# Turning all dS units by DMA and giving one dS product in sixteen to GpSimd

## The chip, the cores and the metric

The kernel runs on one core of a Trainium2 chip. A core has a matrix engine (TensorE, "PE"), three engines for elementwise work (VectorE "DVE", ScalarE "ACT", GpSimd "POOL"), a queue engine that here only issues transfers (SyncE, "SP"), and 16 DMA engines that carry out the transfers of all queues. The metric is the device time of one execution in microseconds; a time stands for the median of several runs. A profiled execution adds a record of every instruction and of every DMA packet.

## The reference

The program computes one transformer block and all its gradients. Sequence length 2048, width 512, 32 heads of 16 columns, an MLP of width 1792 with squared ReLU, and six modulation vectors from a condition vector. Cut to what matters here:

```python
def attention(x, wqkv, wo):                    # B=1, S=2048, H=32, Dh=16
    q, k, v = split_heads(x @ wqkv)
    scores = einsum('bhqd,bhkd->bhqk', q, k) * Dh ** -0.5
    p = softmax(scores)
    o = einsum('bhqk,bhkd->bhqd', p, v)
    return merge_heads(o) @ wo

out, vjp = jax.vjp(block, x, wqkv, wo, w1, b1, w2, b2, c, w_mod)
grads = vjp(grad_out)                          # nine gradients
```

The backward pass of attention makes, for each head, the probabilities E again, the product dP = dO V^T, the gradient dS = E * dP (the row terms of the softmax ride along in padded rows of the operands), and from these dV = E^T dO, dK = dS^T Q and dQ = dS K.

## The kernel before

The forward pass and the MLP fill the first 1120 us or so. The change lies in what follows, the backward loop of attention (lines 1554 to 1763).

**Units.** The 32 heads are taken four at a time (8 head groups). A unit is one head group, one chunk of 512 keys (`kc`), one chunk of 512 queries (`qc`), and one tile of 128 of these queries (`qi`); there are 512 units, and four consecutive ones (the four `qi`) are a block, 128 blocks in all. Queries lie on the partitions, keys along the free dimension.

**Steps of a unit.** `score` (line 1588): for each of the four heads, PE multiplies q by k into one PSUM bank of 128x512; three banks, called A, B and C, take turns. `expo` (1598): ACT takes the exponential of that bank into a quarter of `E_u` (bf16, 128x2048; four such buffers). `dp_pair` (1603): for two heads at a time, PE makes dP in the two-bank PSUM tile `psD_u` (two buffers), and DVE multiplies it by E into half of `dS_u` (bf16, 128x2048, six buffers); two such products of 128x1024 make a unit's dS. `k_quad` and `v_quad` (1644, 1653): PE adds dS^T q and E^T dO into the bank `accVK`. `transpose_unit` (1622): SP issues a DMA transpose of the whole `dS_u`, 512 KB, into a quarter of `dsT`, a tile per block (three buffers). `dq_quad` (1669): two blocks later PE multiplies the turned dS by K into `dqacc`, which shares bank C, and `dq_out` (1680) lets ACT copy it and POOL add it to the dQ of the head group.

**The fourth unit of every second block.** For blocks with odd number (`on_pe`), the unit with `qi == 3` is not turned by DMA. Instead `pe_turn` (1636) has PE turn it by 16 matmuls of 128x128 with the identity, eight at a time into `ptT` in bank C, and ACT copies each eight into `dsT` (line 1756, 128x1024). So 448 units are turned by DMA and 64 by PE.

**Order.** The loop is scheduled by hand on all five engines: a string of tokens for each block gives the order in which instructions are issued, and each engine works through its own in that order. `s` is a score, `e` an exp, `D` a `dp_pair`, `q` a `k_quad` or `v_quad` in turn, `d` two `dq_quad`s of the block two back, `Q` its `dq_out`; `t` and `T` are the PE turn and its copy, `f` a dummy matmul on PE (`keep_warm`, 1632). There are two strings: `order_t` in the blocks that follow an odd one, with `t`, `T` and four `f`, and `order_n` in the others. A unit's transpose is issued with its second `D`. `at` hangs the loads of the next head group on ACT's queue, one at every fourth `D`, and, at the end of the loop, five loads on SP's queue.

Of the kernel before, what the change touches and what calls it, by code (L numbers as in the profile page):

```python
# [14 lines left out]
AF = mybir.ActivationFunctionType  # L15
ALU = mybir.AluOpType
AX = mybir.AxisListType
BF = dt.bfloat16
F32 = dt.float32

P = 128
D = 512
# [12 lines left out]
def kernel(  # L35
# [17 lines left out]
    PE = nc.tensor  # L53
    DVE = nc.vector
    ACT = nc.scalar
    POOL = nc.gpsimd
# [5 lines left out]
    identb = persist.tile([P, P], BF, name="identb")  # L62
# [84 lines left out]
    with ExitStack() as ph:  # L147
# [4 lines left out]
        ework = att.enter_context(tc.tile_pool(name="phCe", bufs=4))  # L152
# [1048 lines left out]
        def head_fill(i):  # L1201
            for key in ("k", "v", "q", "do"):
                POOL.memset(hsets[i][key][:], 1.0 if key in ("k", "v") else 0.0)
# [345 lines left out]
    with ExitStack() as ph:  # L1549
        tpool = ph.enter_context(tc.tile_pool(name="phIt", bufs=3))  # L1550
        ework = ph.enter_context(tc.tile_pool(name="phIe", bufs=4))
        wk = ph.enter_context(tc.tile_pool(name="phIw", bufs=2))
        psd = ph.enter_context(tc.tile_pool(name="psId", bufs=2, space=bass.MemoryType.PSUM))
        psx = ph.enter_context(tc.tile_pool(name="psIx", bufs=1, space=bass.MemoryType.PSUM))
        units = [(hg, kc, qc, qi) for hg in range(HG) for kc in range(QC) for qc in range(QC) for qi in range(4)]
        NU = len(units)
        hst, bst, sst, dqt, cur = {}, {}, {}, {}, {}

        def load_head(hg):
            st = dict(hsets[hg % 2])  # L1560
            st["qz"] = qz[hg % 2]
            st["acc"] = stg.tile([P, n], F32, name="dQacc", tag="dQacc", bufs=1)
            st["dq"] = stg.tile([P, n], BF, name="dQst", tag="dQst", bufs=1)
            st["vk"] = stg.tile([P, n], BF, name="vkb", tag="vkb")
            hst[hg] = st
# [22 lines left out]
        def score(u, hq, bank):  # L1588
            hg, kc, qc, qi = units[u]
            st = hst[hg]  # L1590
            qt = qc * 4 + qi
            r = 32 * hq
            psS = psx.tile([P, 512], F32, name=f"psS_{bank}", tag=banks[bank])
            sst[u, hq] = psS
            PE.matmul(psS[:], st["q"][r:r + 32, qt * P:(qt + 1) * P], st["k"][r:r + 32, kc * 512:kc * 512 + 512],  # L1595
                      start=True, stop=True, tile_position=(r, 0))

        def expo(u, hq):
            if hq == 0:
                bst[u] = [ework.tile([P, 4, 512], BF, name="E_u", tag="E_u"), None]  # L1600
            ACT.activation(bst[u][0][:, hq, :], sst.pop((u, hq))[:], AF.Exp, scale=SCALE)  # L1601

        def dp_pair(u, pair):
            hg, kc, qc, qi = units[u]
            st = hst[hg]
            qt = qc * 4 + qi
            if pair == 0:
                bst[u][1] = ework.tile([P, 4, 512], BF, name="dS_u", tag="dS_u", bufs=6)
            E_u, dS_u = bst[u]
            psD = psd.tile([P, 2, 512], F32, name="psD_u", tag="pd")  # L1610
            for hi in range(2):
                r = 32 * (2 * pair + hi)
                PE.matmul(psD[:, hi, :], st["do"][r:r + 32, qt * P:(qt + 1) * P], st["v"][r:r + 32, kc * 512:kc * 512 + 512],  # L1613
                          start=True, stop=True, tile_position=(r, 0))
            DVE.tensor_tensor(dS_u[:, 2 * pair:2 * pair + 2, :], psD[:], E_u[:, 2 * pair:2 * pair + 2, :], ALU.mult)  # L1615
            if qi == 3 and on_pe(u // 4):
                held["dS"] = dS_u

        def on_pe(b):
            return b % 2 == 1  # L1620

        def transpose_unit(u):
            hg, kc, qc, qi = units[u]
            if qi == 0:
                dqt[u // 4] = tpool.tile([P, 4, 16, P], BF, name="dsT", tag="dsT")
            if qi == 3 and on_pe(u // 4):
                return
            SP.dma_start(out=dqt[u // 4][:, qi], in_=bst[u][1].rearrange("p h k -> p (h k)"), transpose=True)

        held = {}  # L1630

        def keep_warm():
            PE.matmul(cur["vk"][0:DH, :], KS_tok[:, 0, D:QPAD], dOs_tok[:, 0, :], start=False, stop=False,
                      tile_position=(0, 0), skip_group_check=True)

        def pe_turn(b, half):
            pt = psx.tile([P, 8, P], BF, name="ptT", tag="px")
            for i in range(8):
                kt = i % 4
                PE.transpose(pt[:, i, :], held["dS"][:, 2 * half + i // 4, kt * P:(kt + 1) * P], identb[:])  # L1640
            dst = dqt[b][:, 3, 8 * half:8 * half + 8, :]
            held[half] = (dst, pt)

        def k_quad(u):
            hg, kc, qc, qi = units[u]
# [34 lines left out]
        def dq_out(b):  # L1680
# [17 lines left out]
                    r = hg % 2 * 64 + hq * DH  # L1698
                    at(cur["j"] + 6 + hq, load, dQc[hg // 2, r:r + DH, :], st["dq"][32 * hq:32 * hq + DH, :])

        order_t = (
# [3 lines left out]
            "s15 q q e15 ").split(), "ABCABBABACABABCA"  # L1705
        order_n = (
            "s0 D s1 q e0 q s2 e1 e2 D s3 s4 q s5 e3 D e4 "
            "e5 s6 q s7 D s8 e6 e7 d1 e8 s9 D d2 e9 q Q s10 "
            "s11 e10 D q s12 e11 e12 s13 e13 D q s14 s15 e14 e15 D q ").split(), "CBACBACBABABCABC"
# [6 lines left out]
        with tc.manual_schedule(engines={PE.engine, ACT.engine, DVE.engine, SP.engine, POOL.engine}):  # L1716
            head_fill(1)
            POOL.memset(qz[1][:], 0.0)
            nD, nq = -1, -4
            idle = psx.tile([P, 512], F32, name="idle", tag="accVK")  # L1720
            for b in range(NU // 4 + 3):
                toks, bank = order_t if on_pe(b - 1) else order_n
                for tok in toks:
                    c, i = tok[0], int(tok[1:] or 0)
                    if c == "s" and b < NU // 4:
                        if i == 0 and units[4 * b][1:] == (0, 2, 0) and units[4 * b][0] + 1 < HG:
                            load_head(units[4 * b][0] + 1)
                        score(4 * b + i // 4, i % 4, bank[i])
                    elif c == "e" and b < NU // 4:
                        expo(4 * b + i // 4, i % 4)  # L1730
                        if b < 2 and i % 2 == 1:
                            if nq > 0:
                                keep_warm()
                            elif nq < 0:
                                PE.matmul(idle[:], ones_bf[:], identb.unsqueeze(1).to_broadcast([P, 4, P]), start=True, stop=True)
                    elif c == "D":
                        if 0 <= nD < 2 * NU:
                            dp_pair(nD // 2, nD % 2)
                            if nD % 2 == 1:
                                transpose_unit(nD // 2)  # L1740
                        nD += 1
                        cur["j"] = nD
                        for j in sorted(j for j in todo if j <= nD):
                            for f, args in todo.pop(j):
                                f(*args)
                    elif c == "q":
                        if 0 <= nq < 2 * NU:
                            (v_quad if nq % 2 else k_quad)(nq // 2)
                        nq += 1
                    elif c == "f" and 0 < nq < 2 * NU:  # L1750
                        keep_warm()
                    elif c == "t" and 0 <= b - 1 < NU // 4:
                        pe_turn(b - 1, i - 1)
                    elif c == "T" and 0 <= b - 1 < NU // 4:
                        dst, pt = held.pop(i - 1)
                        ACT.activation(dst, pt[:], AF.Identity)  # L1756
                    elif c == "d" and 0 <= b - 2 < NU // 4:
                        for kt in (2 * i - 2, 2 * i - 1):
                            dq_quad(b - 2, kt)
                    elif c == "Q" and 0 <= b - 2 < NU // 4:  # L1760
                        dq_out(b - 2)
            assert not todo
        dq_last = hst[HG - 1]["dq"]

    with ExitStack() as ph:
# [15 lines left out]
        order = (("vk", 6), ("vk", 0), ("vk", 1), ("vk", 2), ("vk", 3), ("dq", 0), ("vk", 7), ("dq", 1), ("vk", 4), ("dq", 2), ("vk", 5), ("dq", 3))  # L1781
# [140 lines left out]
        with tc.manual_schedule(engines={PE.engine, ACT.engine, DVE.engine}):  # L1922
            for k, (key, i) in enumerate(order):
                for g in range(2):
                    if (2 * k + g) % 2 == 0:
                        pt = pst.tile([P, 8, P], BF, name="ptq", tag="ptq")
                    else:
                        pt = psd.tile([P, 8, P], BF, name="ptd", tag="pdh1")
                    for ti in range(8):
                        t = 8 * g + ti  # L1930
                        PE.transpose(pt[:, ti, :], xs[key, i][:, t * P:(t + 1) * P], identb[:])
                    if key == "dq":
                        dst = dq_tok[:, 8 * g:8 * g + 8, i * P:(i + 1) * P]
                    else:
                        dst = dvk_tok[:, 8 * g:8 * g + 8, i, :]
# [32 lines left out]
            for b in range(3):  # L1968
                for ic in range(DC):
                    dwqkv(b, ic)  # L1970
                    i = b * DC + ic
# [75 lines left out]
```

## Time and profile before

| What | Value |
|---|---|
| Median of three runs | 2543.87 us (2539.78 to 2545.97) |
| Span of the profiled execution, first to last instruction | 2533.7 us |
| The profiled execution's own time | not listed apart from its span |
| Backward loop, first to last transpose issued | 1126.1 to 2401.7 us |
| PE busy | 2353.2 us, 93% |
| ACT busy | 2305.1 us, 91% |
| DVE busy | 1808.8 us, 71% |
| POOL busy | 348.5 us, 14% |
| Packets of SP's DMA queue (q1) | 81.9% of the 16 engines' span |

The page has the busy share of each engine over the whole span, rows of 40 slices of equal length (63.3 us each) with a digit for the tenths that an engine was busy, the granted clock of PE and the busy share of the DMA engines in the same slices, the DMA queues with their packets, the chain of work that ended last, and the costliest groups of instructions. "SPq" is SP's queue of DMA issues. On DVE and ACT an instruction's listed time begins while the one before it is still draining, so the time an instruction takes from its engine is read from start to start. Further answers of the trace give a line's or a tile's instructions with their shortest, middle and longest time, a timeline of an engine in which like instructions without idle time between them are merged into one piece, the busy times in a stretch, and who waited for whom.

### The profile page before, as it was taken

The page shows a single profiled execution, that of the slowest core. Times are in us where ns is not written, and L with a number is a line of the kernel's source. Part 1 is how long each engine was busy: PE and PEld are TensorE (multiplying, and loading weights), DVE is VectorE, ACT ScalarE, POOL GpSimd, SP SyncE. Part 2 cuts the span into 40 slices and gives each one's busy share as a digit, 9 for nine tenths or more (in the row PEclk, how much of TensorE's full clock was granted, in tenths as well). Part 3 has the DMA queues.
Part 4 walks back from the last instruction along what each step waited for, and adds up shares of the span by engine and source line. Part 5 has one row for each costly group of instructions (what it writes and reads, how often), then busy time and mean ns, then how long its engine had stood idle before and what let it go on. Part 6 is the DMA issues. An engine that isn't in the chain of part 4 may idle for free.

```text
span 2533.7 us, 50560 instructions
## 1 busy us (share of the span) xinstructions
PE 2353.2 (93%) x19005; PEld 777.5 (31%) x19005; DVE 1808.8 (71%) x2317; ACT 2305.1 (91%) x3577; POOL 348.5 (14%) x370
## 2 busy tenths in 40 slices
PE   7898889989988998999999999999999999999999
PEld 3232223223322323533232223232232322332343
DVE  5555153454444455579899999899998998998872
ACT  7999999999999999549999999999999998998952
POOL 2000001211323141110101101011010110100100
PEclk9999999999999999999899999999999999999999
DMA  6477454366649765979999999999999999999972
GB/s 204 126 191 190 140 130 128 90 164 144 94 101 193 129 144 119 276 199 194 189 201 199 198 197 203 197 195 201 206 202 195 202 195 199 202 203 207 200 241 73
DMA packets 1227131, 447.21 MB, mean 177 GB/s; under 512 B 1103096, under 2 KB 1197752, under 8 KB 1226631
## 3 DMA queue, kind: packets, MB, share of 16 engines
q1 hardware_dynamic: 1198966, 409.14, 81.9%
q0 software_dynamic: 10944, 16.78, 4.6%
q10 hardware_dynamic: 16976, 18.07, 2.6%
q8 instruction: 149, 2.44, 0.4%
q14 instruction: 96, 0.78, 0.1%
HBM read 96.75 MB, written 73.95 MB: 67 GB/s over the span
## 4 chain that ended last, share of the span: by engine, by line
PE 41%; ACT 37%; DVE 7%; issue 7%; DMA 5%; SPq 2%; ACTq 0%; POOL 0%; DVEq 0%; POOLq 0%
ACT E_u L1601 23%; ACT ET L562 11%; PE dqacc L1677 5%; PE psST L560 4%; PE psS_A L1595 3%; PE pm L233 3%; DMA dsT<-dS_u 2%; PE accVK L1650 2%; PE oacc L576 2%; PE psS_B L1595 2%; ACT dsT L1756 2%; PE pdh L1871 2%; PE psS_C L1595 2%; SPq L178 2%; PE pm L412 2%
## 5 line engine op out<-in xcount | busy, mean ns | idle before, releaser
L1615 DVE TENSOR_TENSOR dS_u<-psD_u,E_u 128x1024 bf16<-128x1024 f32 x1024 | 1186.1, 1216 | 93.0 <-PE psD_u L1613 27.2
L562 ACT ACTIVATE ET<-psST 128x1024 bf16<-128x1024 f32 x1024 | 942.7, 1240 | 23.4 <-PE psST L560 22.7
L1601 ACT ACTIVATE E_u<-psS_A 128x512 bf16<-128x512 f32 x768 | 507.8, 661 | 14.1 <-DMA out_dram<-xlast 7.2
L1601 ACT ACTIVATE E_u<-psS_B 128x512 bf16<-128x512 f32 x768 | 501.2, 653 | 8.9 <-PE psD_u L1613 2.2
L1613 PE MATMUL psD_u<-iv,ido 32*128 32x512 bf16 x2048 | 412.0, 390 | 5.4 <-DVE dS_u L1615 5.2
L560 PE MATMUL psST<-qt_sb,kt_sb 32*128 32x512 bf16 x2048 | 315.7, 387 | 50.4 <-ACT ET L562 45.5
L1601 ACT ACTIVATE E_u<-psS_C 128x512 bf16<-128x512 f32 x512 | 332.8, 650 | 13.4 <-DMA dsT<-dS_u 9.9
L1595 PE MATMUL psS_A<-ik,iq 32*128 32x512 bf16 x768 | 296.2, 386 | 11.2 <-ACT E_u L1601 1.1
L1595 PE MATMUL psS_B<-ik,iq 32*128 32x512 bf16 x768 | 297.1, 387 | 9.4 <-ACT E_u L1601 1.9
L1595 PEld LDWEIGHTS <-iq 32*128 32x128 bf16 x2048 | 130.0, 91 | 319.1 <-issue 303.4
L1650 PE MATMUL accVK<-dS_u,qz 128*32 128x512 bf16 x2048 | 215.4, 392 | 0.9 <-DVE dS_u L1615 0.6
L576 PE MATMUL oacc<-ET,vaug 128*32 128x512 bf16 x2048 | 207.4, 395 | 3.2 <-DVE ostage L580 3.2
L1659 PE MATMUL accVK<-E_u,dOs_tok 128*16 128x512 bf16 x2048 | 204.6, 388 | 0.0
L1695 POOL TENSOR_TENSOR dQacc<-dQacc,dqtmp 128x512 f32<-128x512 f32 x64 | 81.3, 1270 | 875.5 <-ACT dqtmp L1690 875.5
L1595 PE MATMUL psS_C<-ik,iq 32*128 32x512 bf16 x512 | 195.1, 381 | 4.2
L560 PEld LDWEIGHTS <-kt_sb 32*128 32x128 bf16 x2048 | 85.1, 91 | 339.6 <-issue 319.1
L1677 PE MATMUL dqacc<-dsT,KS_tok 128*32 128x512 bf16 x2048 | 150.1, 392 | 25.2 <-ACT E_u L1601 10.9
L1756 ACT ACTIVATE dsT<-ptT 128x1024 bf16<-128x1024 bf16 x128 | 144.4, 1128 | 10.1 <-PE ptT L1640 9.6
L251 DVE COPY part<-pm 128x512 f32<-128x512 f32 (+2 forms) x103 | 63.4, 616 | 117.6 <-PE pm L233 109.2
L1613 PEld LDWEIGHTS <-ido 32*128 32x128 bf16 x2048 | 105.8, 91 | 105.7 <-issue 99.5
L1650 PEld LDWEIGHTS <-qz 128*32 128x32 bf16 x2048 | 58.9, 94 | 179.2 <-issue 164.9
L576 PEld LDWEIGHTS <-vaug 128*32 128x32 bf16 x2048 | 53.0, 93 | 122.2 <-issue 122.2
(407 smaller groups left out, 2515.4 us busy)
## 6 DMA issues: line engine op xcount, KB each, us to landing
p_st<-part POOLq DMA_DIRECT2D x36, 256.0 KB, 5.2
kt_sb<-qkT_st SPq DMA_DIRECT2D x124, 64.0 KB
wA<-in_B_w_dram SPq DMA_DIRECT2D x28, 256.0 KB
dsT<-dS_u SPq DMA_TRANSPOSE x448
wB<-w1T_st SPq DMA_DIRECT2D x21, 256.0 KB
wA<-w2T_st SPq DMA_DIRECT2D x21, 256.0 KB
wB<-in_B_w_dram SPq DMA_DIRECT2D x21, 256.0 KB
p_st<-part POOLq DMA_DIRECT2D x25, 192.0 KB, 4.2
```

The source lines that it names most:

```text
L560: PE.matmul(ps[:, hi, :], kt_sb[r:r + 32, kt * P:(kt + 1) * P], qt_sb[r:r + 32, :], start=True, stop=True, tile_position=(r, 0))
L562: ACT.activation(ET[:, 2 * pair:2 * pair + 2, :], ps[:], AF.Exp, scale=SCALE)
L576: PE.matmul(oacc[32 * hq:32 * hq + 32, :], lhsT, ET[:, hq, :], start=(kt == 0), stop=(kt == TT - 1), tile_position=(0, 32 * hq), skip_grou ...
L1595: PE.matmul(psS[:], st["q"][r:r + 32, qt * P:(qt + 1) * P], st["k"][r:r + 32, kc * 512:kc * 512 + 512], start=True, stop=True, tile_positi ...
L1601: ACT.activation(bst[u][0][:, hq, :], sst.pop((u, hq))[:], AF.Exp, scale=SCALE)
L1613: PE.matmul(psD[:, hi, :], st["do"][r:r + 32, qt * P:(qt + 1) * P], st["v"][r:r + 32, kc * 512:kc * 512 + 512], start=True, stop=True, til ...
L1615: DVE.tensor_tensor(dS_u[:, 2 * pair:2 * pair + 2, :], psD[:], E_u[:, 2 * pair:2 * pair + 2, :], ALU.mult)
L1650: PE.matmul(cur["vk"][32 * hq:32 * hq + 32, :], hst[hg]["qz"][:, qt, hq, :], bst[u][1][:, hq, :], start=(qt == 0), stop=False, tile_positi ...
L1659: PE.matmul(acc[32 * hq:32 * hq + DH, :], dOs_tok[:, qt, (hg * 4 + hq) * DH:(hg * 4 + hq + 1) * DH], E_u[:, hq, :], start=False, stop=(qt ...
L1677: PE.matmul(acc[32 * hq:32 * hq + 32, :], KS_tok[:, kc * 4 + kt, h * DH:h * DH + 32], tT[:, :, hq * 4 + kt, :], start=(kt == 0), stop=(kt ...
L1695: POOL.tensor_tensor(dst2, dst, tmp[:], ALU.add)
L1756: ACT.activation(dst, pt[:], AF.Identity)
```

## The change

All 512 units are now turned by DMA. `on_pe`, `held`, `pe_turn`, the tokens `t`, `T` and `f` and the string `order_t` go; every block uses what was `order_n`.

In every eighth unit (`u % 8 == 4`), the product of the first head pair is not made by DVE. It is put aside (`spread`), and behind the next exp in the string ACT copies its `psD_u` out of PSUM into a new bf16 tile `dP_u` (two buffers), and POOL multiplies that by E into the first half of `dS_u`. These are 64 of the 1024 products.

```diff
-            DVE.tensor_tensor(dS_u[:, 2 * pair:2 * pair + 2, :], psD[:], E_u[:, 2 * pair:2 * pair + 2, :], ALU.mult)
-            if qi == 3 and on_pe(u // 4):
-                held["dS"] = dS_u
-
-        def on_pe(b):
-            return b % 2 == 1
+            heads = slice(2 * pair, 2 * pair + 2)
+            if u % 8 == 4 and pair == 0:
+                spread.append((psD, E_u, dS_u))
+            else:
+                DVE.tensor_tensor(dS_u[:, heads, :], psD[:], E_u[:, heads, :], ALU.mult)
+
+        spread = []
+
+        def spread_pair():
+            psD, E_u, dS_u = spread.pop()
+            dP = ework.tile([P, 2, 512], BF, name="dP_u", tag="dP_u", bufs=2)
+            ACT.activation(dP[:], psD[:], AF.Identity)
+            POOL.tensor_tensor(dS_u[:, 0:2, :], dP[:], E_u[:, 0:2, :], ALU.mult)

         def transpose_unit(u):
...
-            if qi == 3 and on_pe(u // 4):
-                return
             SP.dma_start(out=dqt[u // 4][:, qi], in_=bst[u][1].rearrange("p h k -> p (h k)"), transpose=True)
...
-        def pe_turn(b, half):
-            pt = psx.tile([P, 8, P], BF, name="ptT", tag="px")
-            for i in range(8):
-                kt = i % 4
-                PE.transpose(pt[:, i, :], held["dS"][:, 2 * half + i // 4, kt * P:(kt + 1) * P], identb[:])
-            dst = dqt[b][:, 3, 8 * half:8 * half + 8, :]
-            held[half] = (dst, pt)
...
-        order_t = (
-            "s0 s1 q s2 e0 e1 D s3 D e2 s4 e3 t1 e4 q T1 D "
-            "s5 s6 e5 f f t2 e6 s7 T2 e7 D s8 e8 D f f s9 e9 q q s10 "
-            "s11 e10 D d1 d2 e11 Q q s12 D e12 s13 e13 q s14 D e14 "
-            "s15 q q e15 ").split(), "ABCABBABACABABCA"
-        order_n = (
+        order = (
             "s0 D s1 q e0 q s2 e1 e2 D s3 s4 q s5 e3 D e4 "
             "e5 s6 q s7 D s8 e6 e7 d1 e8 s9 D d2 e9 q Q s10 "
             "s11 e10 D q s12 e11 e12 s13 e13 D q s14 s15 e14 e15 D q ").split(), "CBACBACBABABCABC"
...
-                toks, bank = order_t if on_pe(b - 1) else order_n
+                toks, bank = order
...
                         expo(4 * b + i // 4, i % 4)
+                        if spread:
+                            spread_pair()
...
-                    elif c == "f" and 0 < nq < 2 * NU:
-                        keep_warm()
-                    elif c == "t" and 0 <= b - 1 < NU // 4:
-                        pe_turn(b - 1, i - 1)
-                    elif c == "T" and 0 <= b - 1 < NU // 4:
-                        dst, pt = held.pop(i - 1)
-                        ACT.activation(dst, pt[:], AF.Identity)
```

More of the change, by code (lines that the diff above doesn't have):

```diff
@@ L1625, in transpose_unit @@
                 dqt[u // 4] = tpool.tile([P, 4, 16, P], BF, name="dsT", tag="dsT")
-            if qi == 3 and on_pe(u // 4):
-                return
             SP.dma_start(out=dqt[u // 4][:, qi], in_=bst[u][1].rearrange("p h k -> p (h k)"), transpose=True)
-        held = {}
         def keep_warm():
```

## The prediction, made before the result was known

> **What bounds the kernel now.** I read the page's busy shares first, then its DMA lines, then the backward loop alone, since the change lies only there.
>
> ```profile
> PE   7898889989988998999999999999999999999999
> DVE  5555153454444455579899999899998998998872
> ACT  7999999999999999549999999999999998998952
> PEclk9999999999999999999899999999999999999999
> DMA  6477454366649765979999999999999999999972
> ```
>
> The loop is the right part of these rows, from the first transpose at 1126 us to the last at 2402 us: 128 blocks of four units, so 64 pairs of blocks in 1276 us, 19.9 us a pair. There four resources read nine tenths at once: PE, DVE, ACT and the DMA engines. Busy shares cannot choose between them, so I price each per pair of blocks.
>
> ```profile
> L1615 DVE TENSOR_TENSOR dS_u<-psD_u,E_u 128x1024 bf16<-128x1024 f32 x1024 | 1186.1, 1216 | 93.0 <-PE psD_u L1613 27.2
> L1756 ACT ACTIVATE dsT<-ptT 128x1024 bf16<-128x1024 bf16 x128 | 144.4, 1128 | 10.1 <-PE ptT L1640 9.6
> L1628 SPq DMA_TRANSPOSE dsT<-dS_u x448: 1681/2670/4379, 1126.1 to 2401.7; - x150
> ```
>
> The first two lines are from the costliest groups (busy us, mean ns of one, idle before it), the third from the answer for the transposing line (min/median/max ns). In the timeline of ACT and DVE the instructions of one engine overlap, so what counts is start to start: ten dS products take 11.87 us, 1.19 us each; a 512-wide exp takes 0.48 us; a 1024-wide copy out of PSUM 0.90 us. A pair of blocks holds 16 products (19.0 us of DVE), and on ACT 32 exps, two copies, two dQ copies and half a vK copy (15.4 + 1.8 + 1.0 + 0.2 = 18.4 us). DVE is close to the 19.9 us, ACT 1.5 us below. Now the queue that transposes:
>
> ```profile
> 1298.44 964.97 SPq L1628 DMA_TRANSPOSE dsT<-dS_u  x340
> ```
>
> ```profile
> q1 hardware_dynamic: 706813, 178.20, 112.0%
> q10 hardware_dynamic: 10304, 12.33, 5.0%
> q8 instruction: 69, 1.13, 0.4%
> q14 instruction: 42, 0.34, 0.1%
> ```
>
> The line is from SP's timeline: 340 transposes stand as one piece, with no idle time between them for 965 us, 2.84 us each. The four others are the DMA queues of that same stretch (packets, MB, time of the packets as a share of the 16 engines'): SP's queue q1 alone is over 100%, since packets overlap. Seven transposes a pair at 2.84 us are 19.9 us: exactly the pair. One view speaks against this:
>
> ```profile
> SPq L1628 <- DVE dS_u L1615: 832.5, 387, 4.0
> ```
>
> By the waits, SP's queue would have waited for DVE for most of the loop. But when I set each transpose beside its own dS product, the product was done first: for unit 278 it ended at 1822.0 and its transpose began at 1826.1. This lag grows from nearly zero (1450 us) to 6-7 us (1600 us), and then the chain of waits shows the bill:
>
> ```profile
> 1606.35 6.56 DMA dsT<-dS_u
> ...
> 1622.62 6.85 DMA dsT<-dS_u
> ```
>
> After the second, PE stands 3.7 us before the dQ matmul that reads the late tile, and the lag is back near 1 us. So the transposing queue is the bound, and DVE comes 5% behind it.
>
> **What one transpose costs.** 2.84 us holds other things, which do not grow with the number of transposes. I fitted the start-to-start time of the 397 transposes that had another one ready behind them to what else the DMA engines did meanwhile: 2.46 us for the transpose alone, + 0.73 for each 16 KB instruction fetch (q8), + 0.29 for each fetch on q14, + 0.37 for each 64 KB of ACT's loads and stores (q10). Check on the stretch above: 340 x 2.46 + 188 x 0.37 (12.33 MB) + 69 x 0.73 + 42 x 0.29 = 969 us, against 965. The error of the 2.46 from resampling is 0.03. The ends for this price are the rows' extremes: 1.68 us (shortest issue) and 2.84 (everything counted in). I take 2.46, as undisturbed packets of q1 arrive at 212 in 0.25 us, 2.42 us for the 2048 of a transpose; this is also their rate at 1946-1948 us, where PE, ACT and DVE all stand still, so lighter engines will not speed it up.
>
> The Trainium skill ("DMA: Bandwidth & Descriptors", Latency and other measured facts) gives a DMA transpose 261 GB/s, and more for contiguous data. That would make an estimated 2.0 us for 512 KB, eight of them 16 us, and the change would hide in DVE's time, as in the first rival below: 2461 us. This trace shows 178 MB in 965 us, 185 GB/s, so I do not go by it.
>
> **The change, part by part (per pair of blocks).**
> - Transposes: 7 become 8 on SP's queue. 64 more in all x 2.46 = +157 us, in the queue that bounds. SP's other DMAs in the loop are five loads near the end, queued behind it and unhurried.
> - PE loses 16 transposes of 128x128 and, as one order now serves all blocks, 4 warming matmuls: about 0.55 us for each group of eight and each two warm ones, 2.2 us. PE is not the bound; gain 0 while DMA covers it. It also issues 20 of 180 matmuls and their weight loads fewer. The q8 fetches seem to be PE's: 1.13 MB over the 8747 matmuls and 8743 weight loads of the stretch is 65 bytes for each. So the 91 fetches of the loop become about 81: 10 x 0.73 = -7 us on the queue.
> - ACT loses two copies (1.8 us) and gains one PSUM read 1024 wide, f32 to bf16. The nearest row is the forward exp of that shape, seven in 6.58 us, 0.94 us. Net -0.9 us, off the bound.
> - DVE loses one product in 16: 19.0 becomes 17.8 us, off the bound.
> - POOL gains one 1024-wide bf16 product. Rows to bound it: 128x2048 bf16 took 4.32 us (half: 2.2), the 512-wide f32 add 1.27 us (double: 2.5). I take 2.5. POOL's adds take 1.9 us a pair; it has room. Its reads beside DVE's cost nothing that shows: DVE's products take 1210 to 1226 ns whether POOL adds or not.
> - The new chain for the first half of every eighth unit: PE, then the ACT copy (emitted behind the next exp, so that exp's wait is now ahead of it), then POOL, about 0.5 + 0.9 + 2.5 = 4 us instead of 1.2. Waiting for it: that unit's transpose, and behind it all of SP's queue; and the k matmuls of the unit on PE three products later, with scores and dP behind them. With the transposes several us late, SP reaches the unit later than POOL finishes: cost 0. Without that cover, PE would wait up to 1 us a pair. The PSUM bank is held by ACT for about the time DVE held it.
> - Late next: with the queue at 8 x 2.46 + 2.4 = 22.1 us a pair and DVE at 17.8, PE waits for the last transposed tile before the dQ matmuls of each block, some 2 us each time. At that moment about four units lie ready in the queue (six dS buffers), so it never runs empty.
>
> **Sum.** Queue before: 448 x 2.46 + 220 x 0.37 + 91 x 0.73 + 52 x 0.29 = 1265 us; the trace has 1278, so 13 us of empty queue, most of it in the first 30 us. After: 512 x 2.46 + 81 + 59 + 15 = 1415, and 8 us empty, as the queue fills sooner: 1423. Difference +145 us. The profiled execution's span is 2533.7 us, 10.2 below the 2543.87 us median of the runs; what lies around the span stays. 2543.87 + 145 = 2689 us.
>
> **The rivals.**
> - *The queue is elastic and the added transposes hide* (faster). For it: some issues take 1.68 us, and after a hold-up packets come at 283 in 0.25 us, 1.81 us a transpose. Then DVE bounds: 15 x 1.19 = 17.8 us, with today's 4% of gaps 18.6 a pair, 64 x (19.9 - 18.6) = -83: 2461 us. It decides once a transpose alone costs under 2.19 us (8 x 2.19 + 2.4 = 19.9). Against: the fast packets only follow hold-ups, as a backlog being cleared; 965 us show no stretch that stays fast. Chance 0.05, and 0.05 for a part of it, ending between 2550 and 2655.
> - *PE's clock falls and PE bounds.* The warming matmuls go, and PE will wait in every block.
>
> ```profile
> 1203.60:1213.80 10.20, 10.20 (x66) 2.89 (x66) 6.38 (x7) 7.89 (x14) 0.00 (x0) 0.50 1.19 189
> 1715.60:1722.40 6.80, 6.80 (x45) 1.19 (x43) 4.82 (x5) 4.00 (x8) 0.46 (x1) 0.50 1.21 226
> ```
>
> These are two stretches of the windows view (busy us and count of PE, weight loads, DVE, ACT, POOL; then granted clock): the second follows a PE wait of 0.99 us. At clock 0.50 seven products come in 10.2 us, 23.3 us for 16. Were PE cold all the time, 64 x (23.3 - 22.1) = +77: 2766 us. Against: with 20 matmuls fewer it is nearer 21, under the queue. The skill's page "TensorE: Matmul & The Clock Gate" (Part 1) halves the clock after an idle window of about 3.4 us; here less than 1 us of idle did it, so its rule would make the coming waits harmless and the trace does not. Chance 0.06.
> - *POOL's chain is late on top.* The uncovered 1 us a pair, 64 us: 2753 us. It needs the k matmuls to wait when the dQ matmuls did not. Chance 0.04.
>
> **How the numbers follow.** The forecast has 0.80. Its own range is 0.06 us, twice the fit's error, times 512: 2658 to 2720. I reach a little further, to 2655 and 2740, to take in part of the cold-clock and POOL cases; this leaves out about 0.18. 0.3% of this kernel, about what can be told from no change, is 7.6 us. Faster 0.05, same 0.02, slower 0.93, since all cases but the first are slower by far more.
>
> **What would show it.** SP's timeline as one piece of over 500 transposes at 2.76 us; PE's dQ matmuls waiting for DMA in nearly every block; DVE's and ACT's gaps up to 4 us a pair; POOL's product near 2.5 us with nobody long waiting for it. The prediction is wrong if SP's queue shows idle time, which would mean shorter transposes than I priced or an empty queue behind POOL, or if the granted clock stays near 0.5.

## The result, and the profile after

The changed kernel takes 2704.88 us (median; 2704.36 to 2708.16) against 2541.82 us for the kernel before in the same comparison: a ratio of 1.0651, with a 95% interval of 1.0627 to 1.0675, 163 us more. (One execution of one experiment below was in a slower state at a lower clock; its ratio leaves it out, its median does not.) Forecast were 2689 us, in a range of 2655 to 2740. The profiled execution has a span of 2706.1 us and took 2708.16 us in all, so only 2.1 us lie around a span.

The 40 slices of the page after:

```profile
PE   8898899989989989988888888888888888888999
DVE  6654344353454545787778787787877877787762
ACT  7999999999999995488888888888888987888843
PEclk9999999999999999877868887777877876698799
DMA  7476563468477659799999999999999999999982
```

In the loop, now from 1128 to 2579 us, DVE and ACT fall from nine tenths to seven or eight. Only the DMA row still shows nine throughout. New is the clock: PE's granted clock, nearly full before, swings between 0.6 and 0.9.

The groups of the products, from the page, and the answers for ACT's copy and for the transposes (min/median/max ns):

```profile
L1619 DVE TENSOR_TENSOR dS_u<-psD_u,E_u 128x1024 bf16<-128x1024 f32 x960 | 1137.1, 1221 | 313.8 <-PE psD_u L1613 242.8
L1627 POOL TENSOR_TENSOR dS_u<-dP_u,E_u 128x1024 bf16<-128x1024 bf16 x64 | 135.8, 2122 | 571.5 <-ACT dP_u L1626 538.3
...
L1626 ACT ACTIVATE dP_u<-psD_u x64: 1018/1055/1055, 1138.9 to 2563.1; 128x1024 bf16<-128x1024 f32 x64
...
L1633 SPq DMA_TRANSPOSE dsT<-dS_u x512: 1632/2575/4435, 1127.8 to 2576.5; - x171
```

DVE's idle time ahead of its products rises from 93 to 314 us, three quarters of it a wait for dP from PE. A single transpose issue takes no longer than before (middle 2.58 us against 2.67); there are simply 64 more. To compare rates I use one stretch for all kernels, 1300 to 2300 us, where the loop runs evenly. Here it is for the kernel before, as DMA queues (packets, MB, share of 16 engines) and issues:

```profile
q1 hardware_dynamic: 728591, 185.65, 111.9%
...
dsT<-dS_u SPq DMA_TRANSPOSE x351
```

and for the changed kernel:

```profile
q1 hardware_dynamic: 740428, 186.68, 109.5%
q10 hardware_dynamic: 10144, 11.84, 4.7%
q8 instruction: 56, 0.92, 0.3%
...
dsT<-dS_u SPq DMA_TRANSPOSE x356
```

351 and 356 transposes in 1000 us, 2.85 and 2.81 us each. The rate has not moved. What has moved is how much work it buys: 351 transposes were 50.1 pairs of blocks, 356 are 44.5.

### The profile page after: what moved, and what is told of

It is laid out like the page before. It is cut to its first block, busy times and chain, and to the rows that moved or that the text cites. A ratio compares the mean times of both kernels' runs of the same rounds, so it can differ in the third digit from the quotient of the medians.

```text
span 2706.1 us, 48208 instructions
## 1 busy us (share of the span) xinstructions
PE 2398.9 (89%) x17724; PEld 698.0 (26%) x17724; DVE 1760.4 (65%) x2253; ACT 2279.9 (84%) x3513; POOL 483.9 (18%) x434
## 5 line engine op out<-in xcount | busy, mean ns | idle before, releaser
L1619 DVE TENSOR_TENSOR dS_u<-psD_u,E_u 128x1024 bf16<-128x1024 f32 x960 | 1137.1, 1221 | 313.8 <-PE psD_u L1613 242.8
L1613 PE MATMUL psD_u<-iv,ido 32*128 32x512 bf16 x2048 | 477.5, 463 | 2.1 <-DVE dS_u L1619 2.0
L1601 ACT ACTIVATE E_u<-psS_C 128x512 bf16<-128x512 f32 x640 | 394.1, 616 | 79.1 <-issue 36.7
L1601 ACT ACTIVATE E_u<-psS_A 128x512 bf16<-128x512 f32 x640 | 398.1, 622 | 44.4 <-PE psD_u L1613 26.3
L1595 PE MATMUL psS_B<-ik,iq 32*128 32x512 bf16 x768 | 356.3, 464 | 51.9 <-ACT E_u L1601 39.5
L1595 PE MATMUL psS_C<-ik,iq 32*128 32x512 bf16 x640 | 278.3, 435 | 103.9 <-ACT E_u L1601 102.2
L1645 PE MATMUL accVK<-dS_u,qz 128*32 128x512 bf16 x2048 | 247.9, 472 | 1.4 <-DVE dS_u L1619 0.9
L1672 PE MATMUL dqacc<-dsT,KS_tok 128*32 128x512 bf16 x2048 | 223.8, 527 | 28.4 <-ACT E_u L1601 15.8
L1627 POOL TENSOR_TENSOR dS_u<-dP_u,E_u 128x1024 bf16<-128x1024 bf16 x64 | 135.8, 2122 | 571.5 <-ACT dP_u L1626 538.3
L1654 PEld LDWEIGHTS <-dOs_tok 128*16 128x16 bf16 x2048 | 49.8, 87 | 157.7 <-issue 157.7
```

The source lines that it names most:

```text
L1619: DVE.tensor_tensor(dS_u[:, heads, :], psD[:], E_u[:, heads, :], ALU.mult)
L1627: POOL.tensor_tensor(dS_u[:, 0:2, :], dP[:], E_u[:, 0:2, :], ALU.mult)
L1645: PE.matmul(cur["vk"][32 * hq:32 * hq + 32, :], hst[hg]["qz"][:, qt, hq, :], bst[u][1][:, hq, :], start=(qt == 0), stop=False, tile_positi ...
L1654: PE.matmul(acc[32 * hq:32 * hq + DH, :], dOs_tok[:, qt, (hg * 4 + hq) * DH:(hg * 4 + hq + 1) * DH], E_u[:, hq, :], start=False, stop=(qt ...
L1672: PE.matmul(acc[32 * hq:32 * hq + 32, :], KS_tok[:, kc * 4 + kt, h * DH:h * DH + 32], tT[:, :, hq * 4 + kt, :], start=(kt == 0), stop=(kt ...
```

## The experiments

Each was timed against the kernel before on the same chip. "Loop" below means first transpose issued to last transpose issued and done by SP; a block's length is the time from its first exp to that of the next block, the middle value over 50 pairs.

**Transposes alone.** All of the kernel before, and the 64 added transposes at their place, into a tile that nobody reads:

```diff
             if qi == 3 and on_pe(u // 4):
+                spare = tpool.tile([P, 16, P], BF, name="spare", tag="spare", bufs=2)
+                SP.dma_start(out=spare[:], in_=bst[u][1].rearrange("p h k -> p (h k)"), transpose=True)
                 return
```

> The kernel before, with the fourth unit of every odd block also turned by DMA, at the place where the change does it, but into a tile that nothing reads; PE still turns it and ACT still copies it, and the warming matmuls stay. Queue theory (the transposing queue bounds, 2.46 us for each transpose): 64 more cost about 157 us, so 2690 to 2715 us. Clock theory (the change is slow because PE, without the turning and warming matmuls, falls to a granted clock of some 0.78 in the loop): PE's work is untouched, so at most 20 us more, below 2565 us.

Measured: 2703.98 us, ratio 1.0648 (1.0624 to 1.0673), 166 us more. Its queue in the same stretch:

```profile
q1 hardware_dynamic: 734577, 185.21, 111.0%
...
dsT<-dS_u SPq DMA_TRANSPOSE x309
spare<-dS_u SPq DMA_TRANSPOSE x45
```

309 + 45 = 354 transposes in 1000 us, the same rate again. The transposes by themselves cost what the whole change costs. The clock theory, which allowed 20 us, falls as the cause of this: PE kept its turning and warming matmuls. The granted clock fell here too, to 0.88 over the loop from 0.97 before, so it can fall without any change to PE's own work.

**Products alone, on the changed kernel.** All 1024 by DVE, otherwise as changed:

```diff
-            if u % 8 == 4 and pair == 0:
+            if False:
```

> The changed kernel, with all 1024 products by DVE again: no ACT copy of dP, no product by POOL. Queue theory: the products do not matter, 2695 to 2715 us as with the change. POOL theory (the chain ACT, POOL, SP is late by about 1 us in each pair of blocks): 64 us less, 2640 us.

Measured: 2693.12 us, ratio 1.0610 (1.0587 to 1.0632). That is some 10 us under the change (the ratio is 0.4% lower), with intervals that still overlap. 360 transposes in the stretch. The products by POOL cost nearly nothing here, as forecast.

**Products alone, on the kernel before.** The ACT copy and the POOL product put into the kernel before:

```diff
+            heads = slice(2 * pair, 2 * pair + 2)
+            if u % 8 == 4 and pair == 0:
+                spread.append((psD, E_u, dS_u))
+            else:
+                DVE.tensor_tensor(dS_u[:, heads, :], psD[:], E_u[:, heads, :], ALU.mult)
...
                         expo(4 * b + i // 4, i % 4)
+                        if spread:
+                            spread_pair()
```

> The kernel before, with one product in sixteen by ACT and POOL as in the change, and nothing else: 448 DMA transposes, 64 turns by PE. Queue theory: DVE is relieved but the queue bounds, so 2535 to 2550 us, no difference that can be told. If DVE were the bound: 64 products of 1.19 us less, 2465 us. POOL theory: 64 us more, 2605 us.

Measured: 2609.94 us, ratio 1.0267 (1.0233 to 1.0302), which is 68 us more and close to what the POOL theory had. My queue theory said no difference and is wrong on this point: taking 64 products off DVE did not leave the kernel where it was, it made another chain longer than the queue.

**The changed kernel without its added transposes.**

```diff
+            if qi == 3 and u // 4 % 2 == 1:
+                POOL.memset(dqt[u // 4][:, qi], 0.0)
+                return
             SP.dma_start(out=dqt[u // 4][:, qi], in_=...)
```

> The changed kernel with the fourth unit of every odd block not turned at all: POOL fills its part of the turned tile with zeros instead (1.8 us of POOL each), so that part of dQ is left out of the computation. 448 DMA transposes, no turning or warming matmuls. Queue theory: the loop returns to what 448 transposes cost, 2530 to 2560 us, whatever the clock. Clock theory: PE has the same work and the same lack of warming as in the change, so it stays above 2660 us.

Measured: 2650.45 us, ratio 1.0434 (1.0396 to 1.0472). Neither theory had this, though the clock theory's 2660 us is near. With 448 transposes the queue is no longer full:

```profile
q1 hardware_dynamic: 668348, 168.51, 99.5%
...
dsT<-dS_u SPq DMA_TRANSPOSE x323
```

323 in 1000 us, where 355 are possible. Something else holds the loop, 110 us above the kernel before. Two candidates were left: the POOL chain and the clock.

**The same, all products by DVE** (`if False:` as above):

> As the run with 64 transposes left out (POOL fills that part of the turned tiles with zeros, so that part of dQ is not computed), but with all products by DVE. It tells what held that run at 2650 us where the queue did not. If the chain over ACT and POOL: back to 2530 to 2560 us. If the lower clock, from the one order for all blocks without warming: it stays at 2620 to 2650 us.

Measured: 2566.3 us, ratio 1.0112 (1.0077 to 1.0146). So 80 to 90 of the 110 us went with the chain over ACT and POOL; the granted clock rose with it, from 0.82 to 0.88. The windows of the two kernels, without and then with DVE making all products (span of the stretch, then busy us and count of PE, weight loads, DVE, ACT, POOL, then granted clock, DMA share, GB/s):

```profile
1300.00:2300.00 1000.00, 870.27 (x7365) 209.75 (x7364) 814.70 (x692) 863.86 (x1635) 280.34 (x166) 0.82 1.05 182
```

```profile
1300.00:2300.00 1000.00, 883.78 (x7941) 218.70 (x7940) 922.98 (x795) 882.80 (x1713) 198.48 (x131) 0.88 1.14 196
```

**The same, kept warm.** Six `keep_warm` tokens (`f`) put into the order of every block:

```diff
-            "s0 D s1 q e0 q s2 e1 e2 D s3 s4 q s5 e3 D e4 "
-            "e5 s6 q s7 D s8 e6 e7 d1 e8 s9 D d2 e9 q Q s10 "
-            "s11 e10 D q s12 e11 e12 s13 e13 D q s14 s15 e14 e15 D q ").split(), ...
+            "s0 D s1 q e0 q s2 e1 e2 D f s3 s4 q s5 e3 D f e4 "
+            "e5 s6 q s7 D f s8 e6 e7 d1 e8 s9 D d2 e9 q Q f s10 "
+            "s11 e10 D q f s12 e11 e12 s13 e13 D q f s14 s15 e14 e15 D q ").split(), ...
```

> The same, with six warming matmuls in every block. If the clock held the runs with transposes left out: granted clock above 0.95 in the loop, and 2530 to 2560 us, where DVE (1.19 us for each of 1024 products) or the 448 transposes bound. If warming cannot be had this way: as without it.

Measured: 2563.44 us, ratio 1.0072 (1.0043 to 1.0100), at a clock of 0.99 in the stretch instead of 0.88. The clock rose as hoped and the time did not follow. That does not clear the clock, since the dummy matmuls take time themselves: of the blocks at full clock, those with them take 10.2 and 9.8 us (middle values of even and odd blocks), those without 9.4 and 9.2. What holds these two runs 20 to 30 us above the kernel before stays open.

**The changed kernel, kept warm**, with the same tokens and everything else as changed:

> The changed kernel with six warming matmuls in every block (about 1.6 us of PE), in the places where it waits least. Queue theory: the 512 transposes alone need some 1425 us, so the loop can only give back what of the 1451 us the queue stood empty: 2675 to 2705 us, at a higher granted clock. Clock theory (the lower clock sets the time): 2640 us or less.

Measured: 2716.39 us, ratio 1.0677 (1.0659 to 1.0694); not faster than the change, and 11 us above the range that the queue theory gave it. The stretch of the changed kernel, and then of this one:

```profile
1300.00:2300.00 1000.00, 865.30 (x7087) 204.16 (x7087) 785.67 (x664) 832.92 (x1572) 192.94 (x116) 0.79 1.15 200
```

```profile
1300.00:2300.00 1000.00, 871.56 (x7610) 242.47 (x7608) 785.93 (x664) 839.99 (x1571) 192.37 (x115) 0.92 1.16 199
```

The clock goes from 0.79 to 0.92, and DVE makes the same 664 products in both. In the trace most blocks now run at full clock in about 10.2 us, faster than the 11.2 us that the queue needs for a block's four transposes. So the transposes fall behind, up to 10 us, until blocks of 14 to 20 us (21 of 122) wait for them, and the lag starts anew. With the clock mostly up, the queue alone holds the kernel to the same rate. A low clock is thus not needed for the slowdown; what part it has in the changed kernel as it stands comes below.

**How far behind the queue the next limit lay before.** The kernel before, and in the even blocks the fourth unit not turned either:

```diff
                 return
+            if qi == 3:
+                POOL.memset(dqt[u // 4][:, qi], 0.0)
+                return
```

> The kernel before, with the fourth unit of the even blocks not turned (POOL fills its part with zeros, so that part of dQ is not computed): 384 DMA transposes, everything else as before. It asks how far behind the queue the next limit lies. Queue theory: the queue needs 64 x 2.46 = 157 us less and no longer bounds; then the blocks run at their own middle lengths, 10.8 us with a turn by PE and 8.5 us without, 19.3 for a pair instead of 19.9 on average: 2505 us. If the queue did not bound before: no difference.

Measured: 2511.0 us, ratio 0.9880 (0.9847 to 0.9912). The queue did bound before, but by 1.2% only. A pair of blocks takes 19.5 us here, against 19.88.

**Three attempts to gain from it.** More turning by PE:

```diff
         def on_pe(b):
-            return b % 2 == 1
+            return b % 4 != 0
```

> The opposite of the change: the kernel before, with PE turning the fourth unit of three blocks in four instead of one in two, so 416 DMA transposes. Queue theory: 32 x 2.46 = 79 us less on the queue, which then no longer bounds; ACT's two copies in half a block more for each pair bring it to 19.3 us, DVE stays at 19.0: about 19.5 us for a pair instead of 19.9, 2515 us. If the queue was never the bound: ACT's 0.9 us a pair show, 2570 us or more.

Measured: 2617.1 us, ratio 1.0284 (1.0247 to 1.0320). A block with a turn by PE takes 10.8 us and one without 8.5 us, in the kernel before already; my sum over ACT alone missed that difference. With it a pair comes to 1.5 x 10.8 + 0.5 x 8.5 = 20.5 us; the run's pair takes 21.2, and the rest was not settled. Next, DVE instead of ACT for the second copy of the turned unit:

```diff
-                        ACT.activation(dst, pt[:], AF.Identity)
+                        if i == 1:
+                            ACT.activation(dst, pt[:], AF.Identity)
+                        else:
+                            DVE.tensor_copy(dst, pt[:])
```

> The kernel before, with the second of the two copies of a unit turned by PE made by DVE instead of ACT; nothing else. 448 DMA transposes stay, so by the queue theory no difference: 2530 to 2550 us. If the blocks with a turn by PE (ACT's load) bounded: up to 30 us less.

Measured: 2547.45 us, ratio 1.0028 (1.0012 to 1.0045). The block with a turn shrinks from 10.79 to 10.44 us, 22 us in all, and the time does not fall: the queue holds it. Last, this together with `return b % 2 == 1 or b % 8 == 6`:

> The same, with PE turning the fourth unit of five blocks in eight instead of four: 432 DMA transposes. An attempt to beat both kernels: the queue then needs 39 us less, and the blocks, if DVE's copy shortens those with a turn to 10.4 us, need 1.25 x 10.4 + 0.75 x 8.5 = 19.4 us a pair: 2515 to 2525 us. If a block with a turn stays at 10.8 us: 2545 us or more.

Measured: 2548.59 us, ratio 1.0044 (1.0021 to 1.0067). The block did take 10.45 us as hoped, and 432 transposes ease the queue, yet a pair takes 20.03 us on average, 0.56 more than the middle lengths of its blocks add up to (19.47). The kernel before has such a remainder too (19.88 against 19.33), and its trace shows where it lies: in 15 of 122 blocks that take 11.6 to 15.8 us, all but one at a granted clock of 0.63 to 0.89. What starts each of them was not settled. No version tried beats the kernel before with the whole output computed.

## Why the prediction was right, and where it was not

**The bound: right, but two of its lines prove less than I took from them.** Added to a kernel that is otherwise untouched, 64 transposes cost 166 us, and wherever the other engines could go faster, the queue held them. I had leaned on SP's timeline, one piece without idle time. After, it shows the same:

```profile
1127.83 1288.91 SPq L1633 DMA_TRANSPOSE dsT<-dS_u  x455
```

Yet the run with transposes left out, whose queue was not full, has it too:

```profile
1289.17 1021.03 SPq L1636 DMA_TRANSPOSE dsT<-dS_u  x329
```

There the transposes' packets leave 150 us of gaps in the loop, against 54 us before and 67 after, which the merged piece does not show. What did separate the cases is the lag between a product's end and its transpose's start. Its middle value is 7.2 us with spare transposes, 6.8 with all products on DVE, 5.7 kept warm, 3.0 before, 2.4 in the changed kernel, 1.8 with transposes left out and all products by DVE, and nothing with transposes left out. The rate agrees at the ends: 351 to 360 transposes in 1000 us in the first five, 308 to 323 in the runs with three blocks in four turned by PE, with fewer transposes in the kernel before, and with transposes left out. In between (337 to 350, in four other runs) it decides nothing.

The other line that I leaned on was misread. I took PE's wait of 3.7 us at 1630 us for a wait for a late tile. ACT's and PE's lines of that moment, in the kernel before:

```profile
1629.84 0.60 ACT L1601 ACTIVATE E_u<-psS_C 128x512 bf16<-128x512 f32 x1 [3.51 <-DMA dsT<-dS_u]
1630.49 1.90 PE L1677 MATMUL dqacc<-dsT,KS_tok 128*32 128x512 bf16 x16 [3.71 <-ACT E_u L1601]
```

The last tile that these matmuls read had landed at 1622.2 us. PE waited for bank C, which `dqacc` shares with a score, and so for the exp; and the exp stood behind one of ACT's own stores (`dQc<-dQst`). By the trace's semaphore records that store waited for the semaphore that a transpose counted on, the one from 1622.62 to 1629.47. The queue does hold the engines there, but through ACT's DMA issues.

**The price of a transpose: a little low.** I took 2.46 us. The spare transposes lengthen the loop from 1279.0 to 1447.4 us, 2.63 us each; fitting the changed kernel in the same way gives 2.5, with the other terms about as before (0.7, 0.2 to 0.3, 0.35). The range's ends, 1.68 and 2.84, held it.

**The sum: 28 us short in the loop, 12 us too long around it.** Predicted were 1415 us of work for the queue and 8 us empty; its own fit makes the changed loop 1424 us of work, and the loop is 1451 us. So the mis-sized terms are the price (9 us) and the empty time (27 us instead of 8). Against that, I had added the 10.2 us between the span before and the median of the runs. Only 2 us lie around a span, so the profiled execution before was simply some 8 us faster than the median; and the profiled execution after was 3 us slower than its own. Together these bring 28 down to 16; that part of the agreement is luck.

**The instruction fetches: right.** 91 became 81 in the loop.

**The step "PE waits for the last transposed tile in every block": wrong.** The waits of the stretch (total us, times, longest):

```profile
DVE dS_u L1619 <- PE psD_u L1613: 168.6, 205, 4.0
...
PE dqacc L1672 <- DMA dsT<-dS_u: 1.4, 1, 1.4
```

By the waits of the whole loop PE waited 5 us for transposes, DVE 6 us (for a dS buffer to come free) and ACT 13 us (behind its own loads and stores, as above). I had let the other engines run at DVE's 17.8 us a pair up to PE's wait; they do not get there. The changed kernel's blocks are of two kinds, which the same windows view shows:

```profile
2107.70:2117.80 10.10, 8.26 (x84) 2.30 (x80) 8.31 (x8) 9.55 (x19) 4.06 (x3) 1.00 1.33 202
2127.50:2139.80 12.30, 11.45 (x88) 2.41 (x88) 8.46 (x8) 9.88 (x18) 3.39 (x2) 0.60 1.26 196
```

Of 122 blocks, 35 ran at a granted clock above 0.95 and took 9.1 to 10.4 us; 44 ran at a clock below 0.7 and took 12.3 us (middle value). The queue needs 11.2 us for a block's four transposes. So the lag grows in the first kind and shrinks in the second; in stretches of the second kind it reaches zero and the queue stands empty for moments. That is the 27 us, and in small the sign of being wrong that I had named. The changed kernel thus runs where two limits cross: the queue, whose own work comes to 1424 us, and blocks slowed by PE's clock. With transposes left out its pair still takes 21.5 us (POOL's zeros included), 4% less than the 22.5 us here. Whether the waits for the queue start the low clock, or the other waits do, was not settled.

**The POOL step: the cover was right, the uncovered price too low.** Covered by the queue it costs about 10 us, in line with the forecast of nothing. Without the queue's cover I had put it at 1 us a pair, 64 us; the run on the kernel before gives 68 us, where part is still covered, and the two runs with transposes left out some 85 us. What failed is my list of who waits for the new chain: it had the transpose and the k matmuls, and not the exp that runs behind the copy on ACT, for which PE waits. DVE's timeline in the changed kernel, with the idle time before each piece:

```profile
2331.80 4.62 DVE L1619 TENSOR_TENSOR dS_u<-psD_u,E_u 128x1024 bf16<-128x1024 f32 x4 [0.83 <-PE psD_u L1613]
2337.72 1.23 DVE L1619 TENSOR_TENSOR dS_u<-psD_u,E_u 128x1024 bf16<-128x1024 f32 x1 [1.29 <-PE psS_C L1595]
2339.25 1.23 DVE L1619 TENSOR_TENSOR dS_u<-psD_u,E_u 128x1024 bf16<-128x1024 f32 x1 [0.30 <-PE psD_u L1613]
```

and ACT's, PE's and POOL's at the same place:

```profile
2336.53 0.62 ACT L1601 ACTIVATE E_u<-psS_C 128x512 bf16<-128x512 f32 x1
2337.00 1.05 ACT L1626 ACTIVATE dP_u<-psD_u 128x1024 bf16<-128x1024 f32 x1
2337.91 0.64 ACT L1601 ACTIVATE E_u<-psS_B 128x512 bf16<-128x512 f32 x1
```

```profile
2338.60 0.50 PE L1595 MATMUL psS_B<-ik,iq 32*128 32x512 bf16 x1 [0.71 <-ACT E_u L1601]
2338.61 0.54 PE L1613 MATMUL psD_u<-iv,ido 32*128 32x512 bf16 x2
```

```profile
2338.14 2.12 POOL L1627 TENSOR_TENSOR dS_u<-dP_u,E_u 128x1024 bf16<-128x1024 bf16 x1 [5.50 <-ACT dP_u L1626]
```

The copy takes 0.91 us of ACT among the exps, so the exp behind it, of bank B, ends that much later, at 2338.55. PE's next score into bank B waits for it, and the next dP, which PE issues behind that score, starts with it at 2338.61. The bank of dP was not the last wait: it had come free at 2338.05. In the run with transposes left out, too, that dP starts 0.8 us later than where DVE makes all products, mostly behind the same wait of 0.71 us. DVE, which was meant to be relieved, only gains idle time, 1.29 us in place of the product and 0.30 us before the one after, which waits for the late dP; and the block that holds the product takes 11.2 us instead of 9.2 (middle values). About half of these 2.0 us is the wait itself: at full clock such blocks take 10.1 us, so the 1 us of my price holds for the wait alone. But only 5 of 61 did run at full clock, against 43 of 61 where DVE made all products, and the other half goes with the lower clock. DVE saved 1.2 us a pair and the block lost 2.0. That mechanism is read from the traces; no run undid it by itself (with the copy at another place among the exps, say). The product itself takes 2.12 us, a little under the lower of the two rows that I had bounded it by.

**The clock rival: the clock did fall, as its condition said, and it did not decide.** Its mean over the loop is 0.785, against 0.97 before. What I held against this rival was wrong: with 20 matmuls fewer a pair on a cold PE should take nearer 21 us, under the queue, but two blocks at a clock below 0.7 take 24.5 us, above the queue's 22.5. Kept warm, the change is nevertheless as slow, because the queue then holds it.

**The fast rival, an elastic queue: ruled out** by the constant rate of all five kernels.

## What to carry to other kernels

Two halves of a change can each be a loss and still not add up: here 64 transposes alone cost 166 us, the products over ACT and POOL alone 68 us, and both together 163 us, since the smaller loss lies in the shadow of the larger one. When four engines are all above nine tenths, compare what each must do per turn of the loop, in start-to-start times and with the queue's rate in a fixed stretch, not busy shares or an unbroken timeline of issues. Work moved off a busy engine through another in-order engine delays all that stands behind it there; look for who waits for that, and not only at the engine's busy time. And look at the blocks one by one: a middle value can hide that they are of two kinds.

## What the runs showed of the hardware that was not expected

The rate of the 512 KB transposes hardly depends on anything that the engines do: 2.78 to 2.85 us each, all included, at granted clocks from 0.79 to 0.98 and with DVE at 664 to 808 products in the same 1000 us. And PE's clock can fall in a steady loop with short waits alone: in the stretch of the changed kernel PE was busy for 87% of the time and never waited longer than 3.5 us, and the granted clock was 0.79. Six dummy matmuls in each block brought it to 0.92 with the same busy share. Blocks of the same work took 9.1 to 10.4 us at full clock and 12.3 us below 0.7.
